# Half as many filling products on TensorE, and one chunk's query copies moved from ScalarE to VectorE

## The chip, the cores and the metric

The kernel runs on one core of one Trainium2 chip. The metric is the time of one execution on the device, in microseconds (us). The core has five engines that run side by side, each through its own list of instructions in a fixed order: TensorE (PE in the rows, with PEld for its weight loads), VectorE (DVE), ScalarE (ACT), GpSimd (POOL) and SyncE (SP), which here issues DMAs.

## The reference, cut to what matters

Three parts run one after the other. First a gated linear recurrence with complex decays, for 4 batches, 8 heads, 768 steps and 48 features. Then a gated layer, and a layer with a mish-like activation.

```
for t in range(S):
    new_re = ar * S_re - ai * S_im
    new_im = ar * S_im + ai * S_re
    kv = einsum('bhd,bhe->bhde', k[:, :, t], v[:, :, t])
    S_re, S_im = new_re + kv, new_im
    y[:, :, t] = einsum('bhd,bhde->bhe', q[:, :, t], S_re)
...
h = (x @ w1) * (x @ w2) @ w3
x2 = h @ w_out
...
h = x2 @ w_in
g = h * tanh(softplus(h))
out = g @ w_out2
```

## The kernel before

The recurrence is cut into 24 chunks of 128 steps (6 for each batch). Its decays are handled in three groups of 64 time steps; group g serves chunks 8g to 8g+7. Three streams of work are merged into one program, and a scheduler with its own idea of durations then sets the order of each engine's list, so a small edit can move instructions far away from it.

- `bh_stream(g)` normalises the decays, multiplies them up step by step on VectorE (lines 332 and 333, the tiles `t` and `p`), scales keys and queries by them (line 360, `kt`), and writes these to DRAM (`kq_d`). At a group's end `table` makes a small table `mt` of decays over a whole chunk (lines 377 to 383) from products `ps_e` of line 341.
- `ch_stream` works on the chunks. For chunk n, SyncE loads keys and queries back (`tm`, line 442), `tr(n)` transposes them on TensorE into PSUM (`ps_tr`, line 494) and copies them to SBUF (`kf` and `qf`, line 495, two halves of four heads each), `scores(n)` multiplies them (`ps_a`, line 543) and VectorE masks the result (`am`, line 544); `yout(n)` makes the output `ps_y`.
- `m1_all` is the gated layer: 27 products of 512 columns (`pa`, `pb`, `acc`, line 634) for each of 8 blocks of each of 6 token tiles. Token tile i needs chunks 4i to 4i+3.

A third phase, the mish layer, begins at about 626 us. The change does not touch it.

Group 0's table is turned by TensorE (`ps_mt`, line 474). Then, while SyncE loads the second part of the first four chunks, TensorE makes 72 products of the 128x128 identity with itself into `ps_x`, whose result nobody reads (lines 600 to 602). They are here called filling products. A product of two F32 operands appears in the trace as two passes, so they are 144 rows there. Then comes `tr(0)`.

Of the kernel before, what the change touches and what calls it, by code (L numbers as in the profile page):

```python
# [69 lines left out]
def kernel(  # L70
# [23 lines left out]
    V, A, T = nc.vector, nc.scalar, nc.tensor  # L94
# [331 lines left out]
    def ch_stream():  # L426

        HB = 4
# [58 lines left out]
        def tr(n):  # L487
            kf[n] = ch.tile([D2, H, C], F32, tag="kf", name="kf", bufs=1)
            qf[n] = ch.tile([D2, H, C], F32, tag="qf", name="qf", bufs=1)
            for z, dst in ((0, kf[n]), (1, qf[n])):  # L490
                for h0 in range(0, H, HB):
                    ps = at_p.tile([D2, HB, C], F32, tag="at", name="ps_tr")
                    for hh in range(HB):
                        T.transpose(ps[:, hh], tm[n][:, h0 + hh, z], id_sb[0:C, 0:C])  # L494
                    A.copy(out=dst[:, h0:h0 + HB], in_=ps)
                    yield .6

        def upd(n):
# [98 lines left out]
        yield 0.0  # L597
        yield from ready(0)
        ps = at_p.tile([128, 128], F32, tag="at", name="ps_x")
        for _ in range(72):  # L600
            T.matmul(ps, lhsT=id_sb, rhs=id_sb, start=True, stop=True)  # L601
        for n in range(B):
            rows(n, kq_d[0][1])
        yield from tr(0)
        for n in range(N):
            if n % B == 0:
                while left[0] < n // B - 1:
                    yield None
            ahead_of(n)
            am = yield from scores(n)  # L610
            if n + 1 < B:
                yield from tr(n + 1)
            yield from yout(n, am)
            if n + B < N:
                yield from upd(n)
            chunks_done[0] = n + 1
            if n + 1 < N:
                yield from ready(n + 1)
                if n + 1 not in tm:
                    load(n + 1)  # L620
                if B <= n + 2 < N and n + 2 not in tm and (n + 2) // NC in tabs:
                    load(n + 2)
                ahead_of(n)
                if n + 1 >= B:
                    turn(n + 1)
                    yield from tr(n + 1)
# [117 lines left out]

    F = fold_stream()
    CH = ch_stream()
    next(CH)
    M = m1_all()
# [427 lines left out]
```

## Time and profile before

| | us |
|---|---|
| runs | 1036.65, 1039.7 (median), 1041.15 |
| profiled execution | 1039.52 |
| its span, first to last instruction | 1037.5 |
| TensorE busy | 955.7 |
| VectorE busy | 732.9 |
| ScalarE busy | 672.4 |

The busy time is a sum over phases with different limits. Which engine sets the time has to be read stretch by stretch, from the waits and from what stands next in each engine's list. Time stamps are us from the span's start.

### The profile page before, as it was taken

What the parts mean: (1) busy time and instruction counts of PE and PEld (TensorE: products, weight loads), DVE (VectorE), ACT (ScalarE), POOL (GpSimd) and SP (SyncE); (2) the same over time, 40 slices, a digit from 0 to 9 for tenths busy, and PEclk for the clock granted to TensorE, in tenths of its full rate; (3) what the DMA queues carried; (4) which work ended last, traced back from release to release, by engine and by line L of the source; (5) the groups of instructions that cost most, each with busy time, mean ns of one, the idle gap of its engine ahead of it and who ended that gap; (6) DMA issues with size and microseconds to landing.
All of it is one profiled execution on the core that took longest, in us unless ns stands there. A gap on an engine that the chain in (4) does not pass through costs nothing.

```text
span 1037.5 us, 14478 instructions
## 1 busy us (share of the span) xinstructions
PE 955.7 (92%) x5184; PEld 769.3 (74%) x5184; DVE 732.9 (71%) x1434; ACT 672.4 (65%) x1269; POOL 101.8 (10%) x150
## 2 busy tenths in 40 slices
PE   1794299999999999999999999999999999999997
PEld 0452198888788778888888888887787888888875
DVE  6999998999999984543335425888878886465552
ACT  6897788976888745644344517986654667446671
POOL 2223322223222220000000000000000000000000
PEclk9996599999999999999999999999999999999999
DMA  7966767745967664444332302324444331000000
GB/s 285 376 192 194 220 170 201 199 123 131 239 165 194 178 171 124 115 112 110 78 95 84 107 1 77 92 76 128 146 151 168 108 111 62 1 31 1 0 31 34
DMA packets 79168, 131.72 MB, mean 127 GB/s; under 512 B 21392, under 2 KB 49216, under 8 KB 79088
## 3 DMA queue, kind: packets, MB, share of 16 engines
q1 hardware_dynamic: 67920, 93.47, 30.4%
q0 software_dynamic: 11024, 37.12, 13.5%
q8 instruction: 43, 0.70, 0.3%
q14 instruction: 37, 0.30, 0.1%
q10 hardware_dynamic: 144, 0.13, 0.0%
HBM read 98.05 MB, written 28.31 MB: 122 GB/s over the span
## 4 chain that ended last, share of the span: by engine, by line
PE 69%; DVE 9%; ACT 9%; DMA 8%; issue 3%; POOL 0%; SPq 0%; DVEq 0%; ACTq 0%; POOLq 0%
PE ps_o L634 15%; PE ps_h L634 15%; PE pa L634 8%; PE acc L634 8%; PE pb L634 8%; PE ps_a L543 3%; PE ps_tr L494 3%; PE ps_u L503 2%; DMA an<-in_a 2%; PE ps_y L560 2%; PE ps_x L601 2%; PE ps_y L563 2%; DMA fw2l<-in_w3t 1%; DVE ends L868 1%; DMA ws<-z 1%
## 5 line engine op out<-in xcount | busy, mean ns | idle before, releaser
L634 PE MATMUL ps_o<-gh,wuh 128*128 128x512 f32 x288 | 113.9, 399 | 2.6 <-ACT osb L850 2.3
L634 PE MATMUL ps_o<-gl,wuh 128*128 128x512 f32 x288 | 113.6, 395 | 0.3 <-DVE gl L142 0.3
L634 PE MATMUL ps_o<-gh,wul 128*128 128x512 f32 x288 | 113.2, 394 | 0.0
L634 PE MATMUL ps_h<-x2h,wil 128*128 128x512 f32 x288 | 113.0, 392 | 0.0
L634 PE MATMUL ps_h<-x2l,wih 128*128 128x512 f32 x288 | 112.6, 391 | 0.0
L634 PE MATMUL ps_h<-x2h,wih 128*128 128x512 f32 x288 | 112.1, 390 | 0.0
L812 ACT ACTIVATE wb<-ps_h 128x512 f32<-128x512 f32 x96 | 56.0, 597 | 79.1 <-PE ps_h L634 78.8
L634 PE MATMUL pb<-x,w2h 128*128 128x512 f32 x288 | 93.0, 401 | 0.2 <-DVE u L652 0.2
L634 PE MATMUL pa<-x,w1h 128*128 128x512 f32 x288 | 92.8, 401 | 0.3 <-DVE u L652 0.2
L142 DVE TENSOR_TENSOR gl<-hb,gh 128x1024 fp32r<-128x1024 f32 x48 | 58.5, 1221 | 45.6 <-ACT gh L141 45.6
L813 DVE COPY hb<-ps_h 128x512 f32<-128x512 f32 x96 | 64.6, 685 | 33.5 <-ACT wb L812 31.4
L652 DVE TENSOR_TENSOR u<-u,pb 128x512 f32<-128x512 f32 x48 | 32.8, 683 | 60.1 <-PE pb L634 58.7
L141 ACT CAST gh<-hb 128x1024 fp32r<-128x1024 f32 x48 | 50.1, 1044 | 37.4 <-PE ps_o L634 35.3
L649 ACT COPY u<-pa 128x512 f32<-128x512 f32 x48 | 28.1, 585 | 63.4 <-PE pa L634 63.2
L332 DVE TENSOR_TENSOR t<-an,p 128x192 f32<-128x192 f32 x192 | 67.1, 349 | 1.0
L634 PEld LDWEIGHTS ps_o<-gh,wuh 128*128 128x128 f32 x288 | 54.0, 188 | 18.6 <-ACT osb L850 3.1
L634 PEld LDWEIGHTS ps_o<-gl,wuh 128*128 128x128 f32 x288 | 54.1, 188 | 13.5 <-DVE gl L142 0.7
L634 PEld LDWEIGHTS ps_o<-gh,wul 128*128 128x128 f32 x288 | 54.0, 188 | 13.2
L634 PEld LDWEIGHTS ps_h<-x2h,wih 128*128 128x128 f32 x288 | 54.1, 188 | 12.0
L634 PEld LDWEIGHTS ps_h<-x2l,wih 128*128 128x128 f32 x288 | 54.1, 188 | 12.0
L634 PEld LDWEIGHTS ps_h<-x2h,wil 128*128 128x128 f32 x288 | 54.1, 188 | 11.6
L141 ACT CAST uh<-u 128x512 fp32r<-128x512 f32 x48 | 29.6, 616 | 48.8 <-DVE u L652 48.4
(191 smaller groups left out, 2314.2 us busy)
## 6 DMA issues: line engine op xcount, KB each, us to landing
tm<-kq_d SPq DMA_DIRECT2D x32, 384.0 KB
an<-in_a POOLq DMA_DIRECT2D x27, 336.0 KB, 4.9
kqt<-in_kq POOLq DMA_DIRECT2D x27, 336.0 KB, 5.4
kq_d<-kt POOLq DMA_DIRECT2D x26, 336.0 KB, 3.7
kq_d<-kt POOLq DMA_DIRECT2D x52, 168.0 KB, 4.6
raw<-in_w3t SPq DMA_DIRECT2D x21, 384.0 KB
vv<-in_v SPq DMA_DIRECT2D x24, 256.0 KB
raw<-in_win SPq DMA_DIRECT2D x16, 384.0 KB
```

Source lines behind the costliest of these rows:

```text
L141: A.copy(out=hi, in_=raw)
L142: V.tensor_tensor(out=lo, in0=raw, in1=hi.bitcast(F32), op=sub)
L332: V.tensor_tensor(out=t, in0=win2, in1=_bc(pv[:, ::-1], 2, 2), op=mul)
L494: T.transpose(ps[:, hh], tm[n][:, h0 + hh, z], id_sb[0:C, 0:C])
L503: T.matmul(ps[:, h], lhsT=tm[n][:, h, 0], rhs=vt[n][:, h, 0:D], start=True, stop=True)
L543: T.matmul(ps[:, hh], lhsT=kf[n][:, h], rhs=qf[n][:, h], start=True, stop=True)
L560: T.matmul(ps[DP * z:DP * z + DP, p], lhsT=state[:, h], rhs=qf[n][:, h], start=True, stop=False)
L634: T.matmul(ps, lhsT=l, rhs=r, start=first and n == 0, stop=final and n == len(seq) - 1)
L649: A.copy(out=u, in_=pa)
L652: V.tensor_tensor(out=u, in0=u, in1=pb, op=mul)
L812: A.activation(out=wb[:, f % GRP], in_=ps, func=AF.Sigmoid, scale=-1.0)
L813: V.tensor_copy(hb[:, f % 2], ps)
```

## The change

The number of filling products goes from 72 to 36. And in `tr`, for the first chunk alone (`n == 0`), the two halves of the transposed queries (`z == 1`, `qf`) are copied out of PSUM by VectorE and no longer by ScalarE; the keys (`kf`) stay with ScalarE, and so do all copies of later chunks.

```
-                    A.copy(out=dst[:, h0:h0 + HB], in_=ps)
+                    (V.tensor_copy if n == 0 and z else A.copy)(out=dst[:, h0:h0 + HB], in_=ps)
...
-        for _ in range(72):
+        for _ in range(36):
             T.matmul(ps, lhsT=id_sb, rhs=id_sb, start=True, stop=True)
```

The scheduler then orders the lists anew. VectorE's list is the same down to the `p` that follows the last `dec` ahead of the first `am` (chunk 0's masked scores). There it read, before:

```order
L333 TENSOR_TENSOR p<-t 128x96
L273 SCALAR_TENSOR_TENSOR m_1458<-y_1460,m_1458 128x336
L332 TENSOR_TENSOR t<-an,p 128x192
L274 TENSOR_TENSOR an<-an,m_1458 128x7x96
L333 TENSOR_TENSOR p<-t 128x96
L283 SCALAR_TENSOR_TENSOR sq<-y_1460,sq 128x7x48
L332 TENSOR_TENSOR t<-an,p 128x192
L142 TENSOR_TENSOR w1l<-dec,w1h 128x384
L333 TENSOR_TENSOR p<-t 128x96
```

Two more `t` and one more `p` follow, and then the first `am`. In the changed kernel the same place reads:

```order
L333 TENSOR_TENSOR p<-t 128x96
L332 TENSOR_TENSOR t<-an,p 128x192
L273 SCALAR_TENSOR_TENSOR m_1422<-y_1424,m_1422 128x336
L333 TENSOR_TENSOR p<-t 128x96
L274 TENSOR_TENSOR an<-an,m_1422 128x7x96
L495 COPY qf<-ps_tr 96x512 x2
L332 TENSOR_TENSOR t<-an,p 128x192
L283 SCALAR_TENSOR_TENSOR sq<-y_1424,sq 128x7x48
L544 TENSOR_TENSOR am<-ps_a,msk 128x512
```

The two copies stand behind four rows of the decay stream that follow the shared `p`, and the first `am` stands two rows behind them; `w1l`, two `t` and `p` pairs and what follows moved behind it.

ScalarE's list around chunk 0's copies, before:

```order
L264 ACTIVATE sq,flags<-y_1460,cb 128x7x48
L270 ACTIVATE m_1458<-y_1460,cb 128x336
L271 ACTIVATE sq<-y_1460 128x7x48
L141 CAST w1h<-dec 128x384
L495 COPY kf<-ps_tr 96x512 x2
L495 COPY qf<-ps_tr 96x512 x2
L275 ACTIVATE an<-an,sg 128x7x48
```

And in the changed kernel:

```order
L264 ACTIVATE sq,flags<-y_1424,cb 128x7x48
L495 COPY kf<-ps_tr 96x512
L270 ACTIVATE m_1422<-y_1424,cb 128x336
L495 COPY kf<-ps_tr 96x512
L271 ACTIVATE sq<-y_1424 128x7x48
L141 CAST w1h<-dec 128x384
L275 ACTIVATE an<-an,sg 128x7x48
```

The key copies moved up by two and three rows, the query copies are gone.

TensorE's list differs at the filling products (35 in place of 71 behind the second half of `ps_mt`), and stays the same from there to the middle of the chunk stage but for single products that move by some rows. `tr(0)` is followed directly by `scores(0)` in both. The larger difference is at `tr(8)`, the first chunk of group 1, behind `ps_mt` of group 1's table. The rows that end at its 16 transposes, before:

```order
L634 MATMUL pb<-x,w2l 128x512
L634 MATMUL pb<-x,w2h 128x512 x2
L634 MATMUL pb<-x,w2l 128x512
L634 MATMUL pb<-x,w2h 128x512
L494 MATMUL ps_tr<-id_sb,tm 96x128 x16
```

And in the changed kernel:

```order
L634 MATMUL acc<-uh,wol 128x512
L634 MATMUL pa<-x,w1h 128x512 x2
L634 MATMUL pa<-x,w1l 128x512
L634 MATMUL pa<-x,w1h 128x512 x2
L634 MATMUL pa<-x,w1l 128x512
L494 MATMUL ps_tr<-id_sb,tm 96x128 x16
```

Between `ps_mt` and these transposes there stand 34 products of line 634 before and 51 in the changed kernel: 17 more are made ahead of `tr(8)`. Ahead of group 2's `ps_e` (line 341) there stand 9 products fewer than before: 3 of line 634 and 6 small ones of `ps_y`, chunk outputs.

In VectorE's list, ahead of group 1's table, one row each of lines 259, 283, 309 and 324 and four small memsets (lines 287 to 290) of group 2 have moved behind the table. Ahead of group 2's table VectorE has the same rows as before, with two more (`qf`) and one fewer (`xp`, line 579).

## Rows read from the trace of the kernel before

**Rows 1.** Busy time by stretch: from:to, length, each engine (instructions), granted clock.
```profile
126.00:387.00 261.00, 255.70 (x1853) 214.57 (x1854) 242.30 (x610) 203.25 (x505) 66.41 (x96) 0.98 0.69 179
387.00:650.00 263.00, 262.62 (x1540) 218.31 (x1539) 114.44 (x196) 129.07 (x291) 0.00 (x0) 1.00 0.32 90
```

**Rows 2.** The chain that ended last: start, us, what (x how many).
```profile
127.31 18.30 PE ps_x L601 x142
...
180.75 2.07 PE pb L634 x9
```

**Rows 3.** TensorE in order of time: start, us, what, [idle before, ended by].
```profile
145.44 1.92 PE L494 MATMUL ps_tr<-id_sb,tm 128*96 128x128 f32 x16
147.69 2.05 PE L543 MATMUL ps_a<-qf,kf 96*128 96x128 f32 x16 [0.33 <-ACT qf L495]
...
150.88 1.08 PE L494 MATMUL ps_tr<-id_sb,tm 128*96 128x128 f32 x8 [0.27 <-ACT kf L495]
```

**Rows 4.** ScalarE in order of time: chunk 0's four copies.
```profile
146.08 1.07 ACT L495 COPY kf<-ps_tr 96x512 f32<-96x512 f32 x2 [2.09 <-PE ps_tr L494]
147.04 1.08 ACT L495 COPY qf<-ps_tr 96x512 f32<-96x512 f32 x2
```

**Rows 5.** Stretches of `ps_x` alone: length, PE busy (passes), PEld, granted clock, DMA.
```profile
126.00:132.00 6.00, 5.55 (x24) 5.26 (x25) 0.50 0.90 283
132.00:145.50 13.50, 13.50 (x122) 13.41 (x121) 1.00 0.80 214
```

**Rows 6.** SyncE in order of time: its issues of the `tm` loads.
```profile
132.54 4.66 SPq L442 DMA_DIRECT2D tm<-kq_d  x8
```

**Rows 7.** A DMA of the page (last: us to landing); the slowest `tm` load, in the chain.
```profile
kq_d<-kt POOLq DMA_DIRECT2D x26, 336.0 KB, 3.7
264.21 7.85 DMA tm<-kq_d
```

**Rows 8.** VectorE in order of time, from the shared `p` to chunk 0's first `am`.
```profile
143.26 0.25 DVE L333 TENSOR_TENSOR p<-t 128x96 f32<-128x96 f32 x1
143.43 0.50 DVE L273 SCALAR_TENSOR_TENSOR m<-y,m 128x336 f32<-128x336 f32 x1
143.85 0.35 DVE L332 TENSOR_TENSOR t<-an,p 128x192 f32<-128x192 f32 x1
144.12 0.85 DVE L274 TENSOR_TENSOR an<-an,m 128x672 f32<-128x672 f32 x1
144.88 0.25 DVE L333 TENSOR_TENSOR p<-t 128x96 f32<-128x96 f32 x1
...
148.88 0.69 DVE L544 TENSOR_TENSOR am<-ps_a,msk 128x512 f32<-128x512 f32 x1 [1.34 <-PE ps_a L543]
```

**Rows 9.** VectorE's copy out of PSUM (a costliest group); ScalarE's `qf` copies (min/median/max ns).
```profile
L813 DVE COPY hb<-ps_h 128x512 f32<-128x512 f32 x96 | 64.6, 685 | 33.5 <-ACT wb L812 31.4
L495 ACT COPY qf<-ps_tr x48: 564/585/622, 147.0 to 541.8; 96x512 f32<-96x512 f32 x48
```

**Rows 10.** TensorE by stretch: length, busy (instructions), granted clock, DMA.
```profile
42.00:44.00 2.00, 0.00 (x0) 1.00 1.07 348
85.00:88.00 3.00, 0.00 (x0) 0.93 1.04 361
88.00:90.00 2.00, 1.92 (x4) 0.50 0.22 85
```

**Rows 11.** TensorE at group 1's table and at `tr(8)`, in order of time.
```profile
263.74 0.28 PE L474 MATMUL ps_mt<-id_sb,mt 64*96 64x64 f32 x2 [1.10 <-DVE mt L383]
272.19 1.93 PE L494 MATMUL ps_tr<-id_sb,tm 128*96 128x128 f32 x16 [0.24 <-DMA tm<-kq_d]
```

**Rows 12.** VectorE's waits from 126 to 387: total us, times, longest.
```profile
DVE rs L309 <- ACT rv L284: 3.9, 5, 1.9
DVE xp L579 <- ACT xp L578: 2.0, 2, 1.8
DVE ws L525 <- DMA ws<-z: 1.7, 1, 1.7
```

## Prediction

> **What bounds the kernel now.** I read the busy time by stretch first, then the chain that ended last, then each engine in order of time around chunk 0. From 126 us, where the filling products begin, to 387 us, where the last decay table is done, two engines are nearly full: TensorE is busy 255.7 of 261.0 us and VectorE 242.3 [rows 1]. That leaves 5.3 us of idle time on TensorE and 18.7 on VectorE. From 387 to 650 TensorE is busy 262.6 of 263.0 and VectorE less than half [rows 1]. So the end of the kernel moves with TensorE, but a saving on TensorE ahead of 387 survives only as far as VectorE, whose own list doesn't shrink, lets TensorE use it. The chain that ended last runs through 142 of the 144 filling passes for 18.30 us [rows 2], so at this place TensorE does set the pace, and every pass that goes is at first a gain.
>
> **The filling products.** Up to 132.0 us the granted clock is 0.50 (1.2 GHz), and 24 passes took 5.55 us, 0.23 us each; behind that it is 1.00 (2.4 GHz), and 122 passes lie in 13.5 us, 0.111 each [rows 5]. The 72 passes that go are the last ones, all at the full clock: 72 x 0.111 = 8.0 us. The rise at 132.0 stays, since 72 passes are left and only some 25 of them lie ahead of it; the other 47 take 5.2 us. The fill then ends at about 137.3, and `tr(0)`, which began at 145.44 [rows 3], can begin at about 137.4.
>
> **Is its data there?** SyncE issues the eight `tm` loads from 132.54 in 4.66 us [rows 6]; chunk 0's are the first two, out after a quarter of that, at 133.7. The rows give no landing time for them. Below, by a similar transfer, 3.7 us; above, by the slowest `tm` load of the chain, 7.85 [rows 7]: 137.4 to 141.5. I take 137.4. With 16 transposes in 1.92 us [rows 3] `tr(0)` is done between 139.3 and 143.5. Both ends lie ahead of what comes next, so this unknown has no price.
>
> **The query copies on VectorE.** `scores(0)` stands right behind `tr(0)` in TensorE's list and needs `qf`. VectorE takes its rows in order, and the two copies stand behind the shared `p` and four more rows (`t`, `m`, `p`, `an`). None of these wait for TensorE, so an earlier `tr(0)` doesn't bring them forward. From start to start the rows took 0.17 (`p`), 0.42 (`m`), 0.27 (`t`), 0.76 (`an`) and 0.17 for the second `p` [rows 8]: 143.26 + 0.17 + 0.27 + 0.42 + 0.17 + 0.76 = 145.05. The trace has no copy of this shape on VectorE; the nearest is 128x512 out of PSUM, 0.685 us, and ScalarE's of the same shape is 0.585 [rows 9]. I take 0.685; the other end moves the result by 0.1. The first half of `qf` is there at 145.75 and `scores(0)` starts at about 145.8. `kf` doesn't hold it: ScalarE stood idle for 2.09 us ahead of its first copy at 146.08 [rows 4], so from 144.0 on it is free for any copy that it has not made yet, and two end by 145.2.
>
> So `scores(0)` starts 145.8 - 137.4 = 8.4 us behind the start of `tr(0)`, where it was 147.69 - 145.44 = 2.25 [rows 3]. The fill gives 8.0 and a new wait takes 6.15 of it: -1.9 us. What hid VectorE's lateness before is the fill itself.
>
> **The clock.** TensorE now stands idle from about 139.3 to 145.8, 6.5 us. In the trace an idle stretch from 85 to 88 brought the clock down (mean 0.93, and 0.50 for the work behind it), while one of 2 us from 42 to 44 left it at 1.00 [rows 10]. The new gap is far longer than either, so I take it that the clock falls. Then the 16 passes of `scores(0)` cost 0.23 instead of 0.111 each, 1.9 us more. Below, 0, if it doesn't fall; above, the clock stays low as long as it did under the fill, 5.7 us, half of which is lost: 2.9. I take 1.9, because the transposes behind it waited for ScalarE anyway [rows 3]. The Trainium skill, page "TensorE: Matmul & The Clock Gate", section "Why this matters for your kernels", says to avoid long idle gaps between bursts of matmuls, since the clock then goes back to its lower level; that speaks against shortening a fill while the work behind it isn't ready. By this rule the term is +1.9; had the clock no such memory, it would be 0 and the sum 1.9 lower.
>
> **VectorE and ScalarE.** VectorE gets two copies, 2 x 0.685 = +1.4, and loses the wait of 1.34 us ahead of its first `am` [rows 8], since the scores come no later than it does. Net 0.0. ScalarE loses 2 x 0.585 [rows 9], which nobody waits for beyond what is counted.
>
> **What the scheduler moved later.** Group 1's table stands behind fewer VectorE rows, and TensorE comes to `ps_mt` about when it did; its waits there and at `tr(8)`, 1.10 and 0.24 us [rows 11], may go: 0 to -1.3, and I take -1.3. Ahead of group 2's `ps_e` there are 9 fewer products. If VectorE sets that moment, they are still to be made behind it. A product of line 634 takes 2.07 / 9 = 0.23 us [rows 2]; 3 of these make 0.7, and the 6 small ones can't cost more than as many of the large: 0 to +2.1, and I take +0.7.
>
> **Sum.** -8.0 + 6.1 + 1.9 + 0.0 - 1.3 + 0.7 = -0.6 us. The profiled execution took 1039.5 (a span of 1037.5 and 2.0 around it), which gives 1038.9; the runs' median of 1039.7 lies 0.2 higher: **1039.1 us**. About 0.5%, 5.2 us, is what a measurement can tell from no change; the three runs shown lie 4.5 us apart.
>
> **Rivals.**
> *The gain arrives.* If the copies didn't wait, the whole 8.0 would be had up to here: 1031.5. Against it stand VectorE's in-order rows ahead of the copies, none of which the change makes faster. Chance 0.05.
> *VectorE's waits fall away.* With a new order, its three longest later waits, 1.9, 1.8 and 1.7 us [rows 12], two of which hang on ScalarE rows that queue with TensorE's results, may vanish: -5.4 on the engine that lets TensorE go on, 1034.0. For it: VectorE has 18.7 us of idle time. Against: TensorE leads by 1.9 us at most. Chance 0.17.
> *The clock stays down (slower).* If the broken work from 145.8 on, with its waits [rows 3], doesn't lift the clock, each us of it costs half. It is slower than 5.2 us only when the low clock lasts over 2 x (5.2 + 1.9) = 14 us, to 160; at 18 us it is +9.0 - 1.9 = +7.1, 1046.6. Against: the fill lifted it in 5.7 us [rows 5]. Chance 0.12.
> *`tr(8)` behind 17 more products (slower).* They take 17 x 0.23 = 3.9 us. If the table comes no earlier, `tr(8)` starts 3.9 later, VectorE's masked scores wait for it, and with the 2.1 above it is -1.9 + 1.9 + 3.9 + 2.1 = +6.0: 1045.5. Against: those products are useful work done early. Chance 0.08.
> *The new wait eats the gain* (the forecast): 0.58.
>
> **How the numbers follow.** Faster by over 0.5%: 0.05 + 0.17 = 0.22. Slower: 0.12 + 0.08 = 0.20. Within: 0.58. The forecast's own bounds are -1.9 - 1.3 = -3.2 and -1.9 + 2.9 + 2.1 = +3.1, 1036.5 to 1042.8. To leave out no more than 2 in 10, the range reaches into the nearer part of the faster rival (1034.0) and of the slower ones: 1034.0 to 1045.0.
>
> **What would show it.** Right: some 72 rows of `ps_x` that end near 137; `tr(0)` soon behind; a wait of TensorE of 6 to 7 us ahead of the first `ps_a`, ended by VectorE's `qf`; the first `ps_a` near 145.8; a granted clock of 0.50 around it; no wait of VectorE ahead of its first `am`. The first step is wrong if VectorE reaches the copies ahead of the transposes, or if the fill ends elsewhere. The forecast is wrong if the first `ps_a` begins well ahead of 145 and the lead is still there at 387 us, or if the clock is low for more than 14 us.

## The result and the profile after

The changed kernel takes 1051.3 us (median of 6 runs, 1049.9 to 1055.1), the kernel before beside it 1040.3 (6 runs): a ratio of 1.011, with a 95% interval from 1.009 to 1.014. It is slower, by some 11 us, and outside the range of the prediction. One run of one kernel below (e2) took 1400.0 us at a mean granted clock of 0.66 and is left out of its median and ratio. The profiled execution has a span of 1048.7 us against 1037.5. Of these 11.2 us, 8.8 are lost ahead of the mish layer and 2.4 within it (413.9 us in place of 411.5); there all lists are the same, and the sixteen executions read here took 411.5 to 416.1.

Where the time goes is read by noting when the same row starts in both traces. At the end of group 0's table the changed kernel is 1.5 us ahead, which the edit has no part in (it lies ahead of it); at `tr(1)` it is 1.6 ahead, at `tr(7)` 1.9. Then `tr(8)` starts 5.9 us late, the first `ps_a` of chunk 8 7.5 late, the third table 6.6 late, and from 398 us to the mish layer (626.0 before, 634.75 after) everything is 8.7 to 9.1 late. So chunk 0, on which most of the prediction was spent, did what it said, and most of the loss comes more than 120 us behind the edit.

TensorE and the other engines by stretch in the changed kernel (from:to, length, busy time of PE, PEld, DVE, ACT, POOL with instructions, granted clock, DMA share, GB/s):

```profile
126.00:387.00 261.00, 243.52 (x1736) 204.55 (x1736) 240.49 (x595) 201.49 (x501) 62.85 (x90) 0.96 0.68 173
387.00:650.00 263.00, 262.84 (x1544) 217.81 (x1544) 110.53 (x199) 121.00 (x279) 3.15 (x6) 0.99 0.34 93
...
255.00:300.00 45.00, 39.53 (x268) 33.13 (x267) 37.58 (x95) 33.15 (x89) 13.38 (x20) 0.96 0.78 181
300.00:400.00 100.00, 94.47 (x628) 75.81 (x627) 88.42 (x225) 69.11 (x176) 23.94 (x35) 0.95 0.70 174
```

The last two stretches in the kernel before:

```profile
255.00:300.00 45.00, 43.09 (x296) 35.52 (x295) 42.21 (x111) 38.79 (x106) 12.87 (x19) 1.00 0.83 204
300.00:400.00 100.00, 97.31 (x681) 78.96 (x680) 86.67 (x218) 67.61 (x167) 23.94 (x35) 0.98 0.67 170
```

The reader is to see that TensorE's idle time there goes from 1.9 + 2.7 to 5.5 + 5.5 us, +6.4, and that the clock's loss goes from 0 + 2.0 to 1.8 + 5.0 us (each stretch times what its clock lacks to 1.00), +4.8. That makes 11.2, a little more than the 10.7 between the lead of 1.9 and the 8.8 of delay, since some of the low clock falls into idle time. TensorE in order of time, at the places of [rows 3] and [rows 11] and near 383 us:

```profile
125.71 10.71 PE L601 MATMUL ps_x<-id_sb 128*128 128x128 f32 x70
136.26 1.47 PE L494 MATMUL ps_tr<-id_sb,tm 128*96 128x128 f32 x12
140.32 0.64 PE L494 MATMUL ps_tr<-id_sb,tm 128*96 128x128 f32 x4 [2.59 <-ACT kf L495]
144.48 3.75 PE L543 MATMUL ps_a<-qf,kf 96*128 96x128 f32 x16 [3.52 <-ACT an L275]
...
260.72 0.28 PE L474 MATMUL ps_mt<-id_sb,mt 64*96 64x64 f32 x2
...
278.07 3.56 PE L494 MATMUL ps_tr<-id_sb,tm 128*96 128x128 f32 x16 [5.24 <-DMA tm<-kq_d]
...
383.37 0.84 PE L634 MATMUL acc<-uh,woh 128*128 128x512 f32 x2 [1.32 <-DMA x<-xp]
```

The fill ends at 136.3, the new wait ahead of the first `ps_a` is there (2.59 in the middle of `tr(0)` and 3.52 behind it), and `ps_a` runs at the low clock (0.50, 1.2 GHz, from 141.5 to 148.3 us). The row names ScalarE's `an` for the second wait, but `ps_a` does not read it; VectorE's first copy of `qf` ends at about 144.3, and in e1 below the wait is put down to it. At `ps_mt` the wait of 1.10 is gone, as forecast, but at `tr(8)` 0.24 has become 5.24. VectorE (the first five rows answer to [rows 8]):

```profile
142.72 0.25 DVE L333 TENSOR_TENSOR p<-t 128x96 f32<-128x96 f32 x1
142.89 0.85 DVE L274 TENSOR_TENSOR an<-an,m 128x672 f32<-128x672 f32 x1
143.66 1.27 DVE L495 COPY qf<-ps_tr 96x512 f32<-96x512 f32 x2
...
146.56 0.69 DVE L544 TENSOR_TENSOR am<-ps_a,msk 128x512 f32<-128x512 f32 x1 [0.95 <-PE ps_a L543]
147.17 0.25 DVE L333 TENSOR_TENSOR p<-t 128x96 f32<-128x96 f32 x1
...
282.75 0.36 DVE L332 TENSOR_TENSOR t<-an,p 128x192 f32<-128x192 f32 x1 [6.69 <-ACT an L276]
```

The last row shows how far the late load reaches: VectorE, the engine that lets TensorE go on up to 387 us, stands still for 6.69 us. It waits for ScalarE's `an`, and ScalarE's list says why:

```profile
273.65 0.56 ACT L275 ACTIVATE an<-an,sg 128x336 f32<-128x336 f32 x1
279.16 0.58 ACT L495 COPY kf<-ps_tr 96x512 f32<-96x512 f32 x1 [4.96 <-PE ps_tr L494]
...
282.15 0.57 ACT L276 ACTIVATE an<-an,sg 128x336 f32<-128x336 f32 x1
```

The second half of `an` stands behind the copies of chunk 8, which wait for the transposes, which wait for the load. One late load stops three engines.

### The profile page after: what moved, and what is told of

Same layout as the page of the kernel before. It is cut to its first block, busy times and chain, and to the rows that moved or that the text cites. A ratio compares the mean times of both kernels' runs of the same rounds, so it can differ in the third digit from the quotient of the medians.

```text
span 1048.7 us, 14332 instructions
## 1 busy us (share of the span) xinstructions
PE 954.1 (91%) x5112; PEld 766.8 (73%) x5112; DVE 735.6 (70%) x1436; ACT 671.8 (64%) x1267; POOL 101.8 (10%) x150
## 4 chain that ended last, share of the span: by engine, by line
PE 69%; DVE 12%; ACT 9%; DMA 7%; issue 2%; POOL 0%; DVEq 0%; SPq 0%; ACTq 0%; POOLq 0%
PE ps_h L634 17%; PE ps_o L634 16%; PE pb L634 8%; PE pa L634 7%; PE acc L634 7%; PE ps_a L543 4%; PE ps_tr L494 3%; PE ps_u L503 2%; PE ps_y L560 2%; DMA raw<-in_w 2%; PE ps_y L563 2%; DVE t L332 1%; DVE kt L360 1%; DVE p L333 1%; DMA an<-in_a 1%
## 5 line engine op out<-in xcount | busy, mean ns | idle before, releaser
L634 PEld LDWEIGHTS pa<-x,w1h 128*128 128x128 f32 x288 | 53.0, 191 | 12.6 <-issue 1.5
```

Source lines behind the costliest of these rows:

```text
L634: T.matmul(ps, lhsT=l, rhs=r, start=first and n == 0, stop=final and n == len(seq) - 1)
```

## The experiments

The program allows edges between neighbours of one engine's list that fix their order and wait for nothing. With them a kernel can be given the lists of another: "held" below.

```
+    for places in lists:
+        last = None
+        for x in places:
...
+                if last is not None:
+                    tc.add_manual_dep(
+                        i, last.name,
+                        mybir.DependencyInfo(mybir.DependencyClass.NoSync, mybir.DependencyReason.DATA), reason="pinned",
+                    )
+                last = i
```

Line numbers of held kernels are 4 higher (`tr` is L498). All runs in one table. The wait at `tr(8)` (none: under 0.2 us), the mean granted clock from 376 to 396 us and the start of the mish layer are from the one profiled execution of each (mish layer: first `ps_h`); the ratio, with its 95% interval, is over the runs.

| kernel | lists | fills | `qf` copies | ratio to before (interval) | wait at `tr(8)` | clock 376:396 | mish layer from |
|---|---|---|---|---|---|---|---|
| before | old | 72 | ScalarE | 1 | 0.24 | 0.91 | 625.98 |
| changed | new | 36 | VectorE | 1.0112 (1.0087 to 1.0138) | 5.24 | 0.74 | 634.75 |
| c1 | old, held | 72 | ScalarE | 0.9993 (0.9969 to 1.0016) | none | 1.00 | 622.80 |
| c2 | new, held | 36 | VectorE | 1.0104 (1.0078 to 1.0130) | 3.15 | 0.74 | 637.25 |
| e1 | old, held | 36 | VectorE | 1.0025 (1.0004 to 1.0045) | 0.37 | 1.00 | 626.12 |
| k1 | old, held | 36 | ScalarE | 1.0016 (0.9998 to 1.0035) | 0.38 | 0.74 | 628.78 |
| k2 | old, held | 72 | VectorE | 1.0022 (1.0002 to 1.0041) | 0.43 | 1.00 | 624.75 |
| e2 | new, held | 72 | VectorE | 1.0102 (1.0078 to 1.0127) | 2.92 | 1.00 | 633.01 |
| h6 | new | 0 | VectorE | 1.0075 (1.0049 to 1.0100) | 1.97 | 0.74 | 631.92 |
| e3 | a third order | 36 | ScalarE | 1.0063 (1.0041 to 1.0085) | 2.28 | 0.83 | 629.36 |
| e4 | a fourth order | 72 | VectorE | 1.0063 (1.0040 to 1.0085) | 3.65 | 0.83 | 632.39 |
| h1 | new to 250 us, then old | 36 | VectorE | 1.0019 (1.0000 to 1.0039) | none | 1.00 | 625.88 |
| h2 | new, old from 240 to 300 | 36 | VectorE | 1.0072 (1.0044 to 1.0100) | 0.51 | 0.83 | 631.04 |
| k3 | new, `ws` moved on SyncE | 36 | VectorE | 1.0082 (1.0053 to 1.0111) | 4.11 | 0.83 | 633.29 |
| h4 | new, `x_d` and `ws` moved on SyncE | 36 | VectorE | 1.0045 (1.0024 to 1.0067) | none | 0.74 | 631.38 |
| k4 | as h4 to 300 us, then old | 36 | VectorE | 1.0026 (1.0003 to 1.0048) | none | 1.00 | 627.73 |

**Edit or order?** e1 makes the whole edit in the old lists; e2 takes the edit of the fill back in the new lists; e3 and e4 make one half each and leave the order to the scheduler.

> The whole edit (36 filling products, chunk 0's two query copies on VectorE), but the list of each engine is held in the order of the kernel before; the two copies stand on VectorE behind the second p ahead of the first am. Theory 'the lists': the edit itself is worth about -0.6 us, and the loss is all from the order of rows some 120 us later, so the time is 1038 to 1041, the first ps_a starts about 3 us earlier than before, tr(8) waits less than 1 us. Rival 'the edit': the idle gap of TensorE at chunk 0 and the clock that falls in it start the loss, whatever the later order: 1048 to 1052.

```
 lists: those of before, with
+L495 COPY qf<-ps_tr x2 on VectorE behind the second p ahead of the first am
```

> The changed kernel with 72 filling products again; the lists of all engines are held in the order of the changed kernel, and the copies stay on VectorE. Theory 'the lists': 72 passes more ahead of tr(0) shorten its waits but not the loss behind 255 us: 1050 to 1054, with a wait of 4 us or more at tr(8). Rival 'the edit': with the fill back, the gap and the fall of the clock at chunk 0 go, and the time goes back to about 1040.

```
 lists: those of the changed kernel
-        for _ in range(36):
+        for _ in range(72):
```

> 36 filling products, the copies with ScalarE as before; the scheduler orders the lists anew, and they are a third order, in which 42 products stand between ps_mt of group 1 and tr(8) (34 before, 51 in the changed kernel) and no ws transfer stands ahead of chunk 8's loads on SyncE, as before. Theory 'the lists': the wait at tr(8) is under 2 us and the time 1036 to 1045, set by its own order. Rival 'the edit', in the form that fewer filling products cost: 1048 or more.

```
-        for _ in range(72):
+        for _ in range(36):
```

> 72 filling products, the two query copies on VectorE; the scheduler orders the lists anew (39 products between ps_mt of group 1 and tr(8), no ws transfer ahead of chunk 8's loads). Theory 'the lists': 1036 to 1045, with a wait under 2 us at tr(8). Rival 'the edit', in the form that copies on VectorE cost: 1046 or more, the loss there from chunk 0 on.

```
-                    A.copy(out=dst[:, h0:h0 + HB], in_=ps)
+                    (V.tensor_copy if n == 0 and z else A.copy)(out=dst[:, h0:h0 + HB], in_=ps)
```

e1's TensorE shows the same chunk 0 as the changed kernel, gap and low clock included, and no wait at `tr(8)`:

```profile
143.06 1.09 PE L498 MATMUL ps_tr<-id_sb,tm 128*96 128x128 f32 x4 [5.68 <-ACT kf L499]
144.42 3.75 PE L547 MATMUL ps_a<-qf,kf 96*128 96x128 f32 x16 [0.27 <-DVE qf L499]
...
273.55 1.93 PE L498 MATMUL ps_tr<-id_sb,tm 128*96 128x128 f32 x16 [0.37 <-DMA tm<-kq_d]
```

Its mish layer starts at 626.12, but its 1042.8 us lie 1.8 over what I gave it; more of that below. e2, with all 72 products back but the new lists, keeps the loss (1050.1 us), though with a shorter wait at `tr(8)` (2.92) than the 4 that I gave. So the order makes most of the loss; the edit in the old order costs 2 to 3 us by e1's ratio. e3 and e4, at 1046.7 us each, are worse than I gave the order theory, and their waits at `tr(8)`, 2.28 and 3.65, are over the 2 that I gave. e3 is better than its rival too; e4's time lies in its rival's range, but its loss does not begin at chunk 0. Both are still ahead at `tr(7)` (by 1.8 and 1.2 us) and lose it at `tr(8)` and behind, so the place is that of the order theory; what was wrong was the idea that 42 or 39 products ahead of `tr(8)`, with no `ws` ahead of its loads, would be harmless. What they share with the changed kernel is shown under "Why is the load late?".

**Is holding the lists free?** All kernels with the edit or a part of it in the old lists stood about 2 us over before, so two controls hold the lists and change nothing else.

> The kernel before, nothing changed but that its lists are held in their own order by edges between neighbours (one filling product stands behind the second transposition of ps_mt instead of ahead of it). If holding the lists is free, the ratio to before is 1.000 within 0.002, and the 1.7 to 2.6 us by which the kernels in the old lists stand over before belong to the edits. If it is not, the ratio is about 1.002, and the edits are worth nothing measurable in the old lists.

> The changed kernel, nothing changed but that its lists are held in their own order. The same lists as in the changed kernel, so its runs should lie as its runs do (1050 to 1055) if the loss belongs to the lists; with waits at tr(8) of 2 to 5 us and a clock that falls for 0 to 10 us near 384 us, as the kernels with these lists have shown. Should the runs lie at 1047 or less, the way the lists are held matters, and the comparison of lists has to be done among held kernels alone.

It is free: 1039.0 and 1051.1 us, as before and as the changed kernel.

**Which part of the order?** h1 goes over to the old lists at 250 us, h2 has them for the stretch around `tr(8)` alone.

> The changed kernel, its lists held in the changed order up to 250 us and in the order of the kernel before from there on (what was done early in the changed order is left out of the rest). Theory 'the lists': the loss is all in the order behind 250 us, so it goes: wait at tr(8) under 1.5 us, the mish layer begins between 624 and 627 us (626.0 before, 634.75 in the changed kernel), time 1037 to 1042. Rival 'the edit' or the early order: a loss of 5 us or more by 626 us, 1046 or more.

> The changed kernel, its lists held in the changed order up to 240 us, then in the order of the kernel before for what that had begun by 300 us, then in the changed order again. Theory A, the wait at tr(8) and what stands still behind it are the root: that wait is under 1.5 us and the mish layer begins between 626 and 629 us. Theory B, the order between 300 and 400 us costs by itself (waits at copies and at x<-xp, the clock that falls at 384): the wait at tr(8) goes all the same, but the mish layer begins between 630 and 633 us.

```
 h1:  new lists to 250 us | what is left, in the old order
 h2:  new lists to 240 us | what before had begun by 300 us, in the old order | the rest in the new order
```

h1 has no loss against before by the mish layer of its profiled execution (625.88), so all of it comes behind 250 us; its time of 1042.9 us is 0.9 over what I gave. h2 decides for two pieces: the wait at `tr(8)` is down to 0.51, and the mish layer still starts 5.1 us late, in the range that theory B gave. h1 and h2 differ in the main in the order behind some 300 us, and their ratios, 1.0019 and 1.0072, lie clear of each other.

**Why is the load late?** In the changed kernel SyncE issues three `x_d` stores from 257.3 and a `ws` transfer at 265.0 ahead of the `tm` loads, and GpSimd the `kq_d` stores, for which the loads wait, at the same time. SyncE of the changed kernel in order of time, then GpSimd's last store, then the load in the chain that ended last (start, us, what):

```profile
257.34 2.91 SPq L671 DMA_DIRECT2D x_d<-x  x3
264.98 0.60 SPq L520 DMA_DIRECT2D ws<-z  x1
266.54 3.35 SPq L442 DMA_DIRECT2D tm<-kq_d  x4
```

```profile
260.02 1.07 POOL L366 DMA_DIRECT2D kq_d<-kt  x2
```

```profile
267.93 10.00 DMA tm<-kq_d
```

In before the stores' last issue ended at 259.6, the `x_d` stores came at 261.1, behind them, and the loads at 263.3:

```profile
261.14 1.88 SPq L671 DMA_DIRECT2D x_d<-x  x3
263.32 3.51 SPq L442 DMA_DIRECT2D tm<-kq_d  x4
```

```profile
258.57 1.07 POOL L366 DMA_DIRECT2D kq_d<-kt  x2
```

The last two `kq_d` stores (24 KB each) tell what it cost, in median us from issue to landing, first in the changed kernel, then in before:

```profile
kq_d<-kt POOLq DMA_DIRECT2D x2, 24.0 KB, 7.4
```

```profile
kq_d<-kt POOLq DMA_DIRECT2D x2, 24.0 KB, 3.1
```

The slowest load then took 10.00 us, where it took 7.85 [rows 7]; why it took longer itself was not tried. GpSimd's list is the same in both kernels. What moved the `x_d` stores is ScalarE's list: they wait for its copies out of `acc` (line 670), which stand ahead of the decay stream's next `rv` row (line 284) in the changed kernel and start at 256.75, and behind it in before, at 260.55. h4 moves the `x_d` stores and the `ws` transfer behind the loads, k3 the `ws` transfer alone.

> The changed kernel in its own lists, but on SyncE the three x_d stores and the first ws transfer ahead of chunk 8's four tm loads stand behind these loads. Theory 'late in a full queue': the x_d stores share the DMA engines with the kq_d stores for which the loads wait; without them the loads go out some 1.5 to 2 us earlier and land 3 to 5 us earlier, the wait at tr(8) falls from 5.2 to under 2.5 us, and the mish layer begins 2 to 6 us earlier, 629 to 633 us. Rival 'late by VectorE and GpSimd': the kq_d stores are late themselves, and the loads come no more than 1 us earlier; wait at tr(8) over 4 us, 634 us.

> The changed kernel in its own lists, but on SyncE the one ws transfer ahead of chunk 8's four tm loads stands behind them; the three x_d stores stay ahead. If the x_d stores in the DMA queue make the loads late, the wait at tr(8) stays at 2 to 5 us and the time at 1047 to 1051. If the ws transfer, which makes SyncE wait for VectorE, is enough to make them late, the wait falls under 1.5 us as when both were moved, and the time is about 1046.6.

```
 SyncE, changed:  x_d x_d x_d ws tm tm tm tm
 SyncE, k3:       x_d x_d x_d tm tm tm tm ws
 SyncE, h4:       tm tm tm tm x_d x_d x_d ws
```

SyncE, GpSimd's last store and TensorE's `tr(8)` in h4 (whose execution is 2 us later than that of the changed kernel from its start on):

```profile
265.43 3.59 SPq L446 DMA_DIRECT2D tm<-kq_d  x4
269.13 2.92 SPq L675 DMA_DIRECT2D x_d<-x  x3
```

```profile
261.89 1.07 POOL L370 DMA_DIRECT2D kq_d<-kt  x2
```

```profile
274.50 1.47 PE L498 MATMUL ps_tr<-id_sb,tm 128*96 128x128 f32 x12
```

From the end of the last store's issue to the first load it takes 265.43 - 262.96 = 2.5 us; in the changed kernel 266.54 - 261.09 = 5.5. And `tr(8)` no longer waits. In k3, where SyncE's order at this place is that of before again, the first load goes out at 266.56, 5.2 us behind the last store's issue, and the wait stays at 4.11:

```profile
257.64 2.83 SPq L675 DMA_DIRECT2D x_d<-x  x3
266.56 4.09 SPq L446 DMA_DIRECT2D tm<-kq_d  x4
```

```profile
260.32 1.07 POOL L370 DMA_DIRECT2D kq_d<-kt  x2
```

So the `ws` transfer alone does not make the load late; with the `x_d` stores out of the way of the `kq_d` stores it comes in time (the `x_d` stores were not moved alone). The other executions agree. From the last store's issue to the first load it is 2.5 us where the `x_d` stores stand behind the loads (h4, k4), 3.6 to 3.7 where they go out behind the `kq_d` stores (before, c1, e1, k1, k2, h1, h2), and 4.7 to 5.5 where they go out beside them (changed, c2, e2, h6, k3, e3, e4). In the last group alone the wait at `tr(8)` is over 0.6 us, and it is about 2 or more in each; e3 and e4 have no `ws` ahead of the loads. The Trainium skill, page "DMA: Bandwidth & Descriptors", section "Issuing engines are not separate DMA queues", says that transfers from SyncE, ScalarE and GpSimd run on the same 16 DMA engines and interleave; the runs agree, with 5.5 against 2.5 us for GpSimd's stores with and without SyncE's beside them.

**The fill by itself, and both halves in the old lists.** With no filling product at all the scheduler gives exactly the new lists (h6).

> The changed kernel without any filling product; the scheduler gives exactly the lists of the changed kernel, so the number of filling products alone differs (0, not 36). Theory: chunk 0 is set by VectorE's copies, so tr(0) starts when its loads land (137 to 141 us) and the first ps_a within 1 us of 144.5 us; the mish layer begins within 1 us of 634.75 us, time 1049 to 1052. Rival 'the clock': without the fill the granted clock stays at 0.50 longer, transposes and scores take twice as long, tr(1) starts 2 to 4 us later, and 1053 or more.

> The kernel before, every list as it was, with 36 filling products in place of 72 and nothing else. From the rows of before: ScalarE stood idle for 2.09 us ahead of its first copy, so tr(0) comes about 9 us earlier and its copies at most 2 us; the first ps_a starts 1 to 2 us earlier, and VectorE's list takes that back. The mish layer begins within 1 us of 626.0 us, time within 0.3% of before (1037 to 1043). Rival: the gap that is left in TensorE's work costs through the clock, 2 us or more already at tr(2), and 1043 or more.

> The kernel before, every list as it was, 72 filling products, and only the two query copies moved to VectorE (behind the second p ahead of the first am). The copies then wait on VectorE for tr(0), which ends at 147 us: VectorE loses up to 2 us there, and the mish layer begins within 1.5 us of 626.0 us; time within 0.3% of before (1037 to 1043). Rival: what e1 showed over before (+2.5 us) belongs to the copies: 1042 or more here, and k1 equal to before.

```
 h6, lists those of the changed kernel:
-        for _ in range(36):
+        for _ in range(0):
 k1, lists those of before:
-        for _ in range(72):
+        for _ in range(36):
 k2, lists those of before, with the two qf copies on VectorE as in e1:
         for _ in range(72):
```

h6's first `ps_a` starts at 143.83 and `tr(1)` at 147.37, no later than with 36 products, though the clock rose only at 139: chunk 0 is set by the copies. At 1048.4 us it lies somewhat under the 1049 to 1052 that I gave. In its profiled execution the wait at `tr(8)` was 1.97 in place of 5.24, in the same lists, and the mish layer came 2.8 us earlier; whether that holds for its other runs is not shown. k1 and k2 each stand about 2 us over before, like e1: no half of the edit gains anything in the old lists. k1 missed what I gave in two places: its first `ps_a` came 3.8 us earlier and not 1 to 2, and its mish layer 2.8 us late, by a fall of the clock at 378 us of which the last section speaks.

**Both pieces taken out.** k4 is h4 up to 300 us with the old lists behind it.

> The changed kernel with both pieces of the loss taken out: its own lists with the x_d stores and the ws transfer moved behind chunk 8's loads up to 300 us, and the order of the kernel before for all that had not begun by then. Theory 'two pieces' (the wait at tr(8), and the waits and the clock's fall between 340 and 395 us that come with the new order there): no wait over 1 us at tr(8), no fall of the clock over 4 us near 380, the mish layer begins between 623.5 and 626.5 us, time 1037 to 1042, no worse than before and perhaps better by up to 2 us. Rival: the order before 300 us leaves its debt to whatever follows, and the mish layer begins at 629 us or later.

```
 k4:  new lists, SyncE as in h4, to 300 us | what is left, in the old order
```

It was ahead by 2.0 us at `tr(10)` and lost that in the change of lists near 300 us (waits of 1.11 and 1.59, and a clock of 0.50 from 304.5 to 307.9). Its mish layer (627.73) lies between what the theory and the rival gave. At 1042.9 us it is no better than e1, and no version with the edit beats the kernel before.

## Why the prediction was wrong

**The step that failed** is "What the scheduler moved later", -1.3 + 0.7 = -0.6 us. It measured +10.7 from `tr(7)` to the mish layer in the profiled execution. The step counted the waits that might go (the one at `ps_mt` did) and the nine products that might lie behind, and took TensorE's and VectorE's lists for the whole. It let the wait at `tr(8)` only shrink and put nothing on a load that comes later, though [rows 11] showed that the wait there was ended by a DMA. The new SyncE list with its `ws` ahead of the loads could be read, but k3 shows that it was not that: the `x_d` stores, released earlier by ScalarE, go out beside the `kq_d` stores for which the loads wait; the last of these land in 7.4 us where it was 3.1, and TensorE waits 5.24 us where it was 0.24. Behind that the new order adds waits and a longer fall of the clock from 300 to 395 us. The rival "`tr(8)` behind 17 more products" named the right place and gave it 0.08. Its mechanism was wrong as well: TensorE made the 17 products ahead of `tr(8)` and then still waited 5.24 us. The load was late, and the queue of products was not.

The loss has two pieces. The wait at `tr(8)`: taking it out in h4 gave back some 7 us by the ratios (1.0112 to 1.0045) and 3.4 us by the mish layer in the profiled executions, of which h4's is 2 us late from its start on. The stretch from 300 to 395 us: h2 goes from 1.4 us behind at chunk 11's scores to 5.1 behind at the mish layer, and h4 from 1.4 ahead (316.5 us) to 5.4 behind. In the changed kernel about half of that is longer waits (5.5 us against 2.7) and half the clock: from 376 to 396 us the clock is 0.74 in the changed kernel, h4, h6 and c2, and 0.91 in before. e2 has the new lists without a fall there (1.00) and loses nothing between chunk 12's scores (+7.4) and chunk 15's (+6.4); its profiled execution is the fastest of its three runs. The order makes the fall likely and does not fix it. The wait for `acc` near 380 us is 1.09 in all seven executions with the old order behind 300 us, and the clock is under 0.9 in one of them (k1). It is 1.19 to 3.16 in the nine others, and the clock is under 0.9 in eight. What in the order makes the later waits longer was not tried one by one and stays open.

**The fill, -8.0.** In size right: the last passes went, `tr(0)` started 9.2 us earlier, of which 1.5 lie ahead of the fill: 7.7 for 8.0.

**The new wait, +6.1 (net -1.9).** Right in kind: the copies on VectorE started at 143.66 (1.27 for two, 0.64 each, where 0.685 was taken) and the first `ps_a` at 144.48 where 145.8 was forecast; less the 1.5 us of lead, that is 0.2 off. But "ScalarE is free for any copy from 144.0 on" hid that its `kf` copies now stand among other rows, and TensorE waited 2.59 us inside `tr(0)`. That cost nothing here, since VectorE came to its copies later still.

**The clock, +1.9.** Right in size: 16 passes took 3.75 in place of 2.05 us. The rule of the Trainium skill that was cited there (page "TensorE: Matmul & The Clock Gate", section "Why this matters for your kernels", on long idle gaps) is borne out: the granted clock is 0.50 from 141.5 to 148.3, with the idle time there in two pieces. How long it stays down was not sure: in e1, the same edit in the old lists, it is 0.50 from 142.5 to 152.7. And the rule does not tell the whole: at 383 us the longest wait was 1.32 us, and the clock fell to 0.50 from 383.8 to 394.1. That fall was not in the sum.

**The sum up to `tr(1)`** was to be 0.0, and measured 0.0 (1.6 us ahead, of which 1.5 come from ahead of the fill). Yet in the old lists the edit costs about 2 us by the ratios (e1, k1 and k2 beside c1). That is 0.2%, and the interval of k1 holds 1.000, so its size is not settled. One reason shows in the control. c1, which is the kernel before in its own lists, made its 144 passes faster than the profiled execution of before, since the clock rose under the fill at 128 and not at 132 us:

```profile
126.00:132.00 6.00, 6.00 (x47) 6.00 (x46) 5.56 (x19) 5.89 (x15) 0.00 (x0) 0.82 0.84 270
```

```profile
125.01 17.86 PE L605 MATMUL ps_x<-id_sb 128*128 128x128 f32 x144
142.71 1.92 PE L498 MATMUL ps_tr<-id_sb,tm 128*96 128x128 f32 x16
144.95 2.05 PE L547 MATMUL ps_a<-qf,kf 96*128 96x128 f32 x16 [0.33 <-ACT qf L499]
146.84 1.04 PE L498 MATMUL ps_tr<-id_sb,tm 128*96 128x128 f32 x8
```

(The first row is of `126:132` and answers to the first of [rows 5]; the others are TensorE in order of time.) Against this execution e1's first `ps_a` is only 0.5 us earlier, and its `tr(1)` 1.1 later, because `ps_a` runs at the low clock (e1's fill starts 0.5 us later). At `tr(2)` e1 is 3.4 behind (157.35 against 153.91), after a clock of 0.50 up to 152.7, and it keeps that to the mish layer (626.12 against 622.80). Part of the gain that was forecast was the late rise of the clock in the one execution that was read, so that the sum up to `tr(1)` came out to 0.0 is in part luck.

**VectorE and ScalarE, 0.0.** The size came out, the reason did not. The wait of the first `am` was to go; it stayed at 0.95 (1.34 before), and the second `am` now waited 0.85. VectorE was 1.5 us ahead at the shared `p`, and 1.75 at the next step's `an` (158.91 against 160.66), so the two copies cost it nothing by then.

**The other rivals.** "The gain arrives" did not come, for the reason given against it. "The clock stays down" did not come at chunk 0 (6.8 us in place of 14); VectorE's waits did not fall away, and a new one of 6.69 us came.

## What to carry to other kernels

Where a scheduler orders the lists, an edit is two changes: what it does, and a new draw of the order for all that follows. Here the first cost some 2 us and the second about 9; four orders of nearly the same work (e3 and e4 hold one half of the edit each) gave 1040, 1047, 1047 and 1051 us. Before a small edit is judged, make it once in the old lists, and read the DMA queues with the same care as the engines' lists: for each load that an engine waited for before, ask which transfers now go out ahead of it or beside the store that it waits for, and which engine's list releases them. The list of one queue alone did not show it here.

## What was not expected of the hardware

The clock fell or stayed behind the same wait in the same lists. The wait for `uh` near 377 us was 1.09 us in before, c1, e1, k1 and k2, and the clock from 376 to 396 us was 0.91, 1.00, 1.00, 0.74 and 1.00. For k1 and k2, whose waits fall into the stretch alike:

```profile
376.00:396.00 20.00, 18.86 (x102) 14.62 (x103) 12.85 (x36) 6.38 (x15) 3.70 (x6) 0.74 0.51 125
```

```profile
376.00:396.00 20.00, 18.88 (x134) 15.25 (x136) 14.31 (x39) 7.57 (x17) 3.70 (x6) 1.00 0.60 155
```

What the clock lacks here, 0.26 x 20 = 5.2 us, thus comes and goes between executions of one list, with no longer wait of TensorE ahead of it; from chunk 14's scores to chunk 15's k1 took 4.6 us longer than k2. It is a good part of why runs of one kernel lie up to 11 us apart: over the 84 runs of before that were made beside the experiments, the span and what the clock lacks in it (the span times one less the mean granted clock, 20.7 to 31.3 us) rise together, with a correlation of 0.83. One profiled execution cannot say what an order is worth there. The other part that was seen lies in the mish layer, which took 411.5 us in before and 416.1 in e1, with the same lists, with waits of TensorE of 0.6 to 1.4 us for copies out of PSUM at other places each time.
